# Blocked attention and two MLPs on one core: global queries of 8 heads in 64x32 tiles, local scores in fp32, keys split 96+128, global tokens in the last block

## The chip, the cores and the metric

The kernel runs on one core of a Trainium2 chip. The metric is device time in microseconds (us), the median of three runs: 881.46 us before (879.99 to 882.30). Engines are named as in the profile: PE (TensorE matmul), PEld (its weight loads), DVE (VectorE), ACT (ScalarE), POOL (GpSimd), SP (SyncE, which issues all loads here).

## What is computed

Four batches, eight heads, 512 local and 32 global tokens of head size 64. Global queries look at all 544 keys, local queries at the 32 global keys and at a window of 32 to each side. Two MLPs with a squared ReLU follow, over 2176 tokens (512 to 2048 to 512).

```
s_g = scale * q_g @ concat(k_g, k_l).T;            out_g = softmax(s_g) @ concat(v_g, v_l)
s_ll = where(|i - j| <= 32, scale * q_l @ k_l.T, -1e9);  s_lg = scale * q_l @ k_g.T
out_l = softmax(concat(s_lg, s_ll)) @ concat(v_g, v_l)
x = concat(out_g, out_l) as (B*S, H*D)
x = relu(x @ w_in)**2 @ w_out      # twice, with moe_* and moe2_* weights
```

## The kernel before

Everything is fp32 in and out. An MLP product is done as three fp32r products (`three`, L568: high x high, high x low, low x high), so each operand is split once into a high fp32r part (ACT) and a low rest (DVE). In this text a triple is one call of `three`.

The 2176 tokens stand in five column blocks of 384, 512, 512, 384 and 384. Blocks 1 and 2 form pair A, 3 and 4 pair B; later stages multiply a pair in a Strassen-like scheme (`products`, `tsums`), block 0 plainly (`first`).

**Attention.** `pair(j)` (L309) does two heads for 256 local queries, 32 times. It loads keys, queries and values, splits keys and queries into fp32r parts (`hk`, `lk`, `hq`, `lq`), and computes scores (L338) for two query tiles t and two heads e in 12 matmuls; the heads lie in rows 0-63 and 64-127 and write two PSUM banks, S0 and S1. DVE adds the mask and takes the row extreme (L350), ACT does exp with a row sum (L355), DVE adds 1e-9 and inverts (L360, L361), and a scaling step (`copy("nm")`, L365) normalises. PE transposes the 224 probabilities as 112+112 (L373), ACT brings them from PSUM (`copy("ev")`), PE multiplies by the values (L386) and `split_out` writes `xh` and `xl`.

`glob(n)` (L404) does the global queries of four heads of one batch, eight times: scores with a 128-wide block-diagonal query operand (L426), maximum (L430), exp (L439), normalisation on POOL (L447), transposes (L452, L456), 20 matmuls with values as the stationary operand (L465).

**First wave.** Once all heads of a block's tokens are there, the first four of 16 hidden chunks of MLP 1 run on it: 32 triples for a block, 160 in all. Their weights are made by `weight` (L480) from 8-byte words. This work fills PE between attention steps. Then come 14 stages of two chunks each; only they hold the rest of the time.

**Order.** `Plan.order` (L131) is a list planner: each step has an engine, a cost, a priority and what it reads and writes; the planner simulates the engines and emits a fixed order for each. Engines run their own order and wait on semaphores. `CFG` holds priorities, buffer counts and which engine takes the turn for a copy (`A`, `D`, `P` for ACT, DVE, POOL, in rotation). A load's priority is its user's less `lead`.

Of the kernel before, what the change touches and what calls it, by code (L numbers as in the profile page):

```python
# [17 lines left out]
S = SG + SL  # L18
# [179 lines left out]
def act(n):  # L198
    return 0.055 + 0.835 * n / 1000
# [7 lines left out]
def kernel(ctx: ExitStack, tc: tile.TileContext, kl, ql, vl, gk, gv, win, wout, msk, idn, out):  # L207
# [101 lines left out]
    def pair(j, prio):  # L309
        u, h2 = divmod(j, H // 2)  # L310
        kb, qb, mb, vb = j % NK, j % NQ, j % NM, j % NV
# [3 lines left out]
        def P():  # L315
# [3 lines left out]
        K, Q, M, ML, HQ, LQ = ("rk", kb), ("rq", qb), ("hk", mb), ("lk", mb), ("hq", mb), ("lq", mb)  # L319
# [3 lines left out]
        load(prio - lead + 0.5, vt[vb], vl[j], 229376, A, (("v", vb),))  # L323
        copy("ck", P(), hk[mb], rk[kb], KW, A + (K,), (M,))
        copy("cq", P(), hq[mb], rq[qb], 256, A + (Q,), (HQ,), scalar=-0.125)
        add("DVE", dve(256), P(), lambda: nc.vector.scalar_tensor_tensor(
            out=lq[mb], in0=rq[qb], scalar=-0.125, in1=hq[mb].bitcast(F32),
            op0=ALU.mult, op1=ALU.subtract), A + (Q, HQ), (LQ,), lock=True)
        minus("lo", P(), lk[mb], rk[kb], hk[mb].bitcast(F32), KW, A + (K, M), (ML,))
        sk = [take("S", CFG["S"]) for _ in range(2)]  # L330

        def scores():
            for t in range(2):
                c, w = slice(128 * t, 128 * t + 128), slice(160 * t, 160 * t + WIN)
                for n, (a, b) in enumerate(((hq, hk), (lq, hk), (hq, lk))):
                    for e in range(2):
                        r = slice(64 * e, 64 * e + 64)
                        nc.tensor.matmul(out=bank[sk[e]][:, t * WIN:(t + 1) * WIN], lhsT=a[mb][r, c], rhs=b[mb][r, w],  # L338
                                         start=n == 0, stop=n == 2)

        add("PE", 0.767, P(), scores, A + (M, ML, HQ, LQ), tuple(sk), mode="S")
# [595 lines left out]
```

## Time and profile before

| | before |
|---|---|
| median of three runs | 881.46 us |
| span of the profiled execution | 877.9 us |
| time outside the span (median less span) | 3.6 us |
| PE / DVE / ACT / POOL busy | 867.1 / 695.6 / 539.4 / 47.7 us |
| attention's last matmul ends | 215.4 us |
| first wave ends, the stages go on | about 248.9 us |

The profile gives the profiled execution's span, from its first to its last instruction, and no other time of it. PE's busy time is not a measure of its load, since matmuls overlap and a matmul that waits inside the pipe counts as busy. How much of a stretch a piece of PE work takes is read from the chain of waits, where each piece stands with the time from the end of the piece before it.

### The profile page before, as it was taken

To read this page: it belongs to the slowest core of one execution; us is meant where nothing else is said; L and a number is where in the kernel's file an instruction comes from. 1 tells how busy PE (TensorE), PEld (TensorE's weight loads), DVE (VectorE), ACT (ScalarE), POOL (GpSimd) and SP (SyncE) were. 2 spreads that over 40 slices of the span, in tenths; PEclk is the share of its full clock that TensorE was granted. 3 is DMA by queue.
4 is the path that set the end of the run, shared out by engine and by line. 5 is a ranking of instruction groups with operands and counts; after the bars stand their busy time and mean duration, and the time that the engine had idled before them with its cause. 6 is when DMAs were issued, how large, how long until landed. Compare 5 with 4: busy or idle time off the path is not lost.

```text
span 877.9 us, 14427 instructions
## 1 busy us (share of the span) xinstructions
PE 867.1 (99%) x5294; PEld 769.4 (88%) x5294; DVE 695.6 (79%) x1657; ACT 539.4 (61%) x1219; POOL 47.7 (5%) x94
## 2 busy tenths in 40 slices
PE   8999999999999999999999999999999999999998
PEld 7777787898889989999889889889988989899896
DVE  4899998832999788897968999788787887895654
ACT  5799999964675456355456678745554545644533
POOL 1232222200000000000000000000000000000000
PEclk9999999999999999999999999999999999999999
DMA  9687355400001121120201002211111111210022
GB/s 300 232 292 252 106 153 162 115 12 1 1 25 49 49 67 53 49 69 29 72 25 49 25 25 72 61 60 49 49 49 49 49 49 48 63 58 25 1 100 104
DMA packets 28070, 67.92 MB, mean 77 GB/s; under 512 B 3168, under 2 KB 13024, under 8 KB 28000
## 3 DMA queue, kind: packets, MB, share of 16 engines
q1 hardware_dynamic: 28000, 67.01, 24.0%
q8 instruction: 41, 0.67, 0.3%
q14 instruction: 29, 0.24, 0.1%
HBM read 62.54 MB, written 4.46 MB: 76 GB/s over the span
## 4 chain that ended last, share of the span: by engine, by line
PE 86%; DVE 6%; ACT 4%; DMA 2%; issue 1%; SPq 0%; ACTq 0%; DVEq 0%
PE h L569 8%; PE h L570 7%; PE h L571 7%; PE PT L570 6%; PE PT L571 6%; PE PT L569 6%; PE S L570 5%; PE S L571 5%; PE S L569 5%; PE Y L569 5%; PE Y L570 4%; PE Y L571 4%; PE O L571 3%; PE O L570 3%; PE O L569 3%; PE O L386 3%
## 5 line engine op out<-in xcount | busy, mean ns | idle before, releaser
L238 DVE TENSOR_TENSOR gl<-r,gh 128x384 fp32r<-128x384 f32 (+1 forms) x160 | 96.2, 607 | 61.7 <-ACT r L593 60.3
L589 ACT ACTIVATE r<-r 128x512 f32<-128x512 f32 (+1 forms) x84 | 48.2, 575 | 94.7 <-DVE r L699 94.4
L570 PE MATMUL PT<-gl,whi 128*128 128x384 f32 (+1 forms) x288 | 103.0, 358 | 0.0
L569 PE MATMUL PT<-gh,whi 128*128 128x384 f32 (+1 forms) x288 | 102.9, 357 | 0.0
L571 PE MATMUL PT<-gh,wlo 128*128 128x384 f32 (+1 forms) x288 | 102.9, 357 | 0.0
L524 ACT ACTIVATE whi<-wt 128x512 fp32r<-128x512 f32 x92 | 57.3, 626 | 65.5 <-DVE wt L500 50.4
L590 ACT ACTIVATE gh<-r 128x384 fp32r<-128x384 f32 (+1 forms) x160 | 89.0, 563 | 5.3 <-issue 1.3
L569 PE MATMUL h<-xh,whi 128*128 128x384 f32 (+1 forms) x244 | 88.9, 364 | 0.6 <-DVE xh L226 0.5
L570 PE MATMUL h<-xl,whi 128*128 128x384 f32 (+1 forms) x244 | 86.2, 353 | 0.0
L571 PE MATMUL h<-xh,wlo 128*128 128x384 f32 (+1 forms) x244 | 86.1, 353 | 0.0
L622 DVE TENSOR_TENSOR y<-y,PT 128x384 f32<-128x384 f32 (+1 forms) x130 | 75.6, 601 | 11.3 <-PE PT L571 11.2
L593 ACT ACTIVATE r<-r 128x384 f32<-128x384 f32 (+1 forms) x145 | 82.1, 570 | 3.6
L569 PE MATMUL Y<-gh,whi 128*128 128x384 f32 (+1 forms) x208 | 76.1, 366 | 0.0
L570 PE MATMUL Y<-gl,whi 128*128 128x384 f32 (+1 forms) x208 | 74.7, 359 | 0.3 <-DVE gl L238 0.3
L571 PE MATMUL Y<-gh,wlo 128*128 128x384 f32 (+1 forms) x208 | 74.3, 357 | 0.0
L238 DVE TENSOR_TENSOR wlo<-wt,whi 128x512 fp32r<-128x512 f32 x92 | 62.5, 685 | 6.7 <-ACT whi L524 6.2
L355 ACT ACTIVATE s<-s,mn 128x224 f32<-128x224 f32 x128 | 60.1, 473 | 10.8 <-DVE mn L350 10.5
L571 PE MATMUL S<-xh,wlo 128*128 128x384 f32 (+1 forms) x172 | 62.0, 360 | 0.0
L570 PE MATMUL S<-xl,whi 128*128 128x384 f32 (+1 forms) x172 | 61.9, 360 | 0.0
L569 PE MATMUL S<-xh,whi 128*128 128x384 f32 (+1 forms) x172 | 61.6, 358 | 0.0
L570 PEld LDWEIGHTS PT<-gl,whi 128*128 128x128 f32 x288 | 54.1, 188 | 4.8
L569 PEld LDWEIGHTS PT<-gh,whi 128*128 128x128 f32 x288 | 54.1, 188 | 4.8
(131 smaller groups left out, 2100.1 us busy)
## 6 DMA issues: line engine op xcount, KB each, us to landing
wraw<-win SPq DMA_DIRECT2D x32, 512.0 KB, 3.6
wraw<-wout SPq DMA_DIRECT2D x32, 512.0 KB, 3.5
v<-vl SPq DMA_DIRECT2D x32, 224.0 KB, 3.1
rk<-kl SPq DMA_DIRECT2D x32, 192.0 KB, 2.8
y<-gk SPq DMA_DIRECT2D x8, 672.0 KB, 4.7
y<-gv SPq DMA_DIRECT2D x8, 640.0 KB, 6.3
rq<-ql SPq DMA_DIRECT2D x32, 128.0 KB, 3.0
out<-y SPq DMA_DIRECT2D x12, 192.0 KB, 1.9
```

Of the source, the lines that this page charges most:

```text
L238: add("DVE", dve(n), prio, lambda: nc.vector.tensor_tensor(out=get(out_), in0=get(a), in1=get(b), op=ALU.subtract), reads, writes, lock=True)
L355: add("Activation", 0.48, P(), lambda t=t, sb=sb: nc.scalar.activation(out=st[sb][:, t, :], in_=st[sb][:, t, :], func=AF.Exp, bias=mn[sb][ ...
L386: nc.tensor.matmul(out=bank[ok][64 * e:64 * e + 64, 128 * t:128 * t + 128], lhsT=vt[vb][:, 128 * k + 64 * e:128 * k + 64 * e + 64], rhs=pt ...
L524: nc.scalar.activation(out=whi[slot], in_=tf, func=AF.Copy)
L569: nc.tensor.matmul(out=out_, lhsT=hi, rhs=xhi, start=start, stop=False, skip_group_check=again)
L570: nc.tensor.matmul(out=out_, lhsT=hi, rhs=xlo, start=False, stop=False, skip_group_check=again)
L571: nc.tensor.matmul(out=out_, lhsT=lo, rhs=xhi, start=False, stop=stop, skip_group_check=again)
L589: add("Activation", act(nb), P(), lambda: nc.scalar.activation(out=r, in_=src, func=AF.Relu), (S,), (R,))
L590: add("Activation", act(nb) + 0.04, P(), lambda: nc.scalar.activation(out=a, in_=r, func=AF.Square), (R,), (("gh", f),))
L593: add("Activation", act(nb) + 0.04, P(), lambda: nc.scalar.activation(out=r, in_=r, func=AF.Square), (), (R,))
L622: add("DVE", dve(nb), P(), lambda: nc.vector.tensor_tensor(out=yd, in0=yd, in1=o, op=ALU.add), (yk[d],), (Y,))
```

## The change

Local attention: keys and queries stay fp32. The four splits and their buffers go; two fp32 matmuls (one for each head) replace six fp32r ones for a query tile. The scale -0.125 moves into the DVE step with the mask, whose values become -8e9. One `sm` buffer for both heads replaces three; DVE adds and inverts once for a pair. The scaling step rotates over `DDDADD` in place of `APA`. Probabilities are transposed as 96+128, the smaller part on 96 rows, and leave PSUM in two ACT copies in place of one. `xh` is always made by ACT.

Global attention: `glob` takes all eight heads of a batch, four times. Scores go as eight 64-row, 32-column tiles into both S banks; the value product has probabilities as the stationary operand (32 columns a head, four side by side) and 64 value columns moving; normalisation is done after it, in the ACT copies from PSUM (L480 of the new file), followed by one more transpose. Keys get own tiles `kg`; only the values still borrow `y` tiles. POOL has no work left.

Layout and plan: block 0 becomes the last columns (last unit and all global tokens). Buffers, priorities and the order of blocks within the first wave (`begin`) and within the stages (`order`) change. `fw` 2 means the same four chunks as before. The number of triples is 1224 in both programs.

```diff
@@ -22,59 +22,58 @@
 UNITS = 8
 NI = UNITS * H
 WIN = 224
+NEAR = 96
 KW = 384
 NEG = 1.0e9
 NB = [384, 512, 512, 384, 384]
-OFF = [0, 384, 896, 1408, 1792]
-UNIT0 = [0] + [384 + 256 * u for u in range(UNITS - 1)]
+OFF = [1792, 0, 512, 1024, 1408]
+UNIT0 = [256 * u for u in range(UNITS)]
 GLOB0 = 256
+GLOB_V = (4, 0)
 PAIRS = {"A": (1, 2), "B": (3, 4)}
...
-CFG = {'warm': 23,
+CFG = {'warm': 27,
- 'nm': 'APA',
+ 'nm': 'DDDADD',
- 'glob': [2, 4, 6, 8, 13, 17, 25, 31],
+ 'glob': [5.9, 15.73, 25.15, 42.23],
- 'lmk': -11.49,
+ 'lmk': -15.028,
- 'NM': 2,
- 'NS': 3,
+ 'NM': 1,
+ 'NS': 5,
- 'xh': 'DDADD',
+ 'xh': 'AA',
- 'begin': [1, 0, 3, 4, 2]}
+ 'begin': [1, 2, 4, 3, 0],
+ 'fw': 2}
...
+    sm = tiles(ap_, "sm", NM, [128, 2, 2])
+    kg = tiles(ap_, "kg", 2, [128, 1152 + S])
+    gmx = ap_.tile([128, 2, 2], F32, name="gmx")
+    gsm = ap_.tile([128, 2], F32, name="gsm")
...
-        copy("ck", P(), hk[mb], rk[kb], KW, A + (K,), (M,))
-        copy("cq", P(), hq[mb], rq[qb], 256, A + (Q,), (HQ,), scalar=-0.125)
-        add("DVE", dve(256), P(), lambda: nc.vector.scalar_tensor_tensor(
-            out=lq[mb], in0=rq[qb], scalar=-0.125, in1=hq[mb].bitcast(F32),
-            op0=ALU.mult, op1=ALU.subtract), A + (Q, HQ), (LQ,), lock=True)
-        minus("lo", P(), lk[mb], rk[kb], hk[mb].bitcast(F32), KW, A + (K, M), (ML,))
+        load(prio - lead + 0.5, vt[vb], vl[j], 262144, A, (("v", vb),))
         sk = [take("S", CFG["S"]) for _ in range(2)]
 
         def scores():
             for t in range(2):
                 c, w = slice(128 * t, 128 * t + 128), slice(160 * t, 160 * t + WIN)
...
+                for e in range(2):
+                    r = slice(64 * e, 64 * e + 64)
+                    nc.tensor.matmul(out=bank[sk[e]][:, t * WIN:(t + 1) * WIN], lhsT=rq[qb][r, c], rhs=rk[kb][r, w],
+                                     start=True, stop=True)
+
+        add("PE", 0.77, P(), scores, A + (K, Q), tuple(sk), mode="S")
...
                     out=st[sb][:, t, :], in0=bank[s][:, t * WIN:(t + 1) * WIN], in1=masks[:, mi, :],
-                    op0=ALU.add, op1=ALU.min, scale=1.0, scalar=3.0e38, accum_out=mn[sb][:, t:t + 1]),
+                    op0=ALU.add, op1=ALU.min, scale=-0.125, scalar=3.0e38, accum_out=mn[sb][:, t:t + 1]),
...
-                    accum_out=sm[sb][:, t:t + 1]), A + (("mn", sb, t),), (("s", sb, t), ("sm", sb, t)))
-
...
+        def tiny():
+            nc.vector.tensor_scalar_add(out=sm[mb], in0=sm[mb], scalar1=1e-9)
+            nc.vector.reciprocal(out=sm[mb], in_=sm[mb])
+
+        add("DVE", 0.3, P(), tiny, A, tuple(("sm", mb, e, t) for e in range(2) for t in range(2)), lock=True)
+        for e in range(2):
+            i = 2 * j + e
+            sb = i % NS
             for t in range(2):
-                copy("nm", P(), st[sb][:, t, :], st[sb][:, t, :], WIN, A + (("sm", sb, t),), (("s", sb, t),),
-                     scalar=sm[sb][:, t:t + 1])
+                copy("nm", P(), st[sb][:, t, :], st[sb][:, t, :], WIN, A + (("sm", mb, e, t),), (("s", sb, t),),
+                     scalar=sm[mb][:, e, t:t + 1])
             tk = take("PT", CFG["PT"])
 
             def trans(sb=sb, tk=tk):
                 for t in range(2):
...
+                    nc.tensor.transpose(bank[tk][:, 256 * t:256 * t + 128], st[sb][:, t, NEAR:WIN], ident)
+                    nc.tensor.transpose(bank[tk][0:NEAR, 256 * t + 128:256 * t + 128 + NEAR],
+                                        st[sb][0:NEAR, t, 0:NEAR], ident[0:NEAR, 0:NEAR])
+
+            add("PE", 0.384, P(), trans, A + (("s", sb, 0), ("s", sb, 1), "ident"), (tk,), mode="T")
             pb = i % NPT
-            copy("ev", P(), pt[pb][0:112, :], bank[tk][0:112, :], 512, A + (tk,), (("pt", pb),), psum=True)
+            two = bank[tk].rearrange("p (t c) -> p t c", t=2)
+            copy("ev", P(), pt[pb][:, :, 0:128], two[:, :, 0:128], 256, A + (tk,), (("pt", pb),), psum=True)
+            copy("ev", P(), pt[pb][0:NEAR, :, 128:128 + NEAR], two[0:NEAR, :, 128:128 + NEAR], 2 * NEAR, A + (tk,), (("pt", pb),), psum=True)
             pbs.append(pb)
 
         def pv():
             for t in range(2):
-                for c in range(2):
+                for n, c in ((128, 1), (NEAR, 0)):
                     k = 2 * t + c
                     for e in range(2):
...
+                        nc.tensor.matmul(out=bank[ok][64 * e:64 * e + 64, 128 * t:128 * t + n],
+                                         lhsT=vt[vb][0:n, 128 * k + 64 * e:128 * k + 64 * e + 64],
+                                         rhs=pt[pbs[e]][0:n, t, 128 - 128 * c:128 - 128 * c + n], start=c == 1, stop=c == 0,
+                                         skip_group_check=True)
+
+        add("PE", 0.817, P(), pv, A + (("pt", pbs[0]), ("pt", pbs[1]), ("v", vb)), (ok,), mode="V")
...
-    def glob(n, prio):
...
+    def glob(bb, prio):
         A = ("arena",)
...
+        K, V = kg, [yflat[b] for b in GLOB_V]
+        GK, GP, GV = [("gk", 0), ("gk", 1)], [("gp", 0), ("gp", 1)], [("gv", 0), ("gv", 1)]
+        p = [k[:, 1152:1152 + S] for k in K]
+        rem, og = K[0][0:32, 512:768], K[1][:, 512:640]
+        ok = CFG["O"][cnt["g"] % len(CFG["O"])]
...
+        for g in range(2):
+            load(prio - 3 + 0.05 * g, K[g][:, 0:1152], gk[2 * bb + g], 589824, A, (GK[g], GP[g]))
+        for g in range(2):
+            load(prio - 2.9 + 0.05 * g, V[g][:, 0:1280], gv[2 * bb + g], 655360, A, (GV[g],))
         for e in range(2):
...
+            sk = [take("S", CFG["S"]) for _ in range(2)]
 
             def scores(sk=sk, e=e):
...
+                for g in range(2):
+                    for j in range(2):
+                        c = 32 * (2 * g + j)
+                        for r in range(2):
+                            rows = slice(64 * r, 64 * r + 64)
+                            nc.tensor.matmul(out=bank[sk[r]][c:c + 32, 0:272], lhsT=K[g][rows, 1088 + 32 * j:1120 + 32 * j],
+                                             rhs=K[g][rows, S * j + 272 * e:S * j + 272 * e + 272], start=True, stop=True)
+
+            add("PE", 0.47, P(), scores, A + tuple(GK), tuple(sk), mode="X")
+            for r in range(2):
+                add("DVE", 0.37, P(), lambda s=sk[r], e=e, r=r: nc.vector.tensor_tensor_reduce(
+                    out=p[r][:, 272 * e:272 * e + 272], in0=bank[s][:, 0:272], in1=zeros, op0=ALU.add, op1=ALU.max,
+                    scale=1.0, scalar=-3.0e38, accum_out=gmx[:, r, e:e + 1]), A + (sk[r], "masks"), (GP[r], "gmx"))
...
+        for r in range(2):
+            add("Activation", 0.75, P(), lambda r=r: nc.scalar.activation(
+                out=p[r], in_=p[r], func=AF.Exp, bias=gmx[:, r, 0:1], scale=0.125, accum_out=gsm[:, r:r + 1]),
+                A + ("gmx",), (GP[r], ("gsm", r)))
...
+        for r in range(2):
+            tk = take("PT", CFG["PT"])
+
+            def trans(r=r, tk=tk):
+                for c in range(4):
+                    nc.tensor.transpose(bank[tk][:, 128 * c:128 * c + 128], p[r][:, 128 * c:128 * c + 128], ident)
+
+            add("PE", 0.436, P(), trans, A + (GP[r], "ident"), (tk,), mode="T")
+            copy("ev", P(), K[r][:, 0:512], bank[tk], 512, A + (tk,), (GK[r],), psum=True)
+        tk = take("PT", CFG["PT"])
+
+        def trans_rem(tk=tk):
+            for r in range(2):
+                nc.tensor.transpose(bank[tk][0:32, 128 * r:128 * r + 128], p[r][:, 512:544], ident)
+
+        add("PE", 0.218, P(), trans_rem, A + (GP[0], GP[1], "ident"), (tk,), mode="T")
+        copy("ev", P(), rem, bank[tk][0:32, 0:256], 256, A + (tk,), (GK[0],), psum=True)
 
         def pv():
...
+            for c0, c1 in ((0, 4), (4, 5)):
+                for r in range(2):
+                    for c in range(c0, c1):
+                        for t in range(4):
+                            g, j = divmod(t, 2)
+                            lhs = K[r][:, 128 * c + 32 * t:128 * c + 32 * t + 32] if c < 4 else rem[:, 128 * r + 32 * t:128 * r + 32 * t + 32]
+                            v = V[g][0:128 if c < 4 else 32, 256 * c + 64 * (2 * j + r):256 * c + 64 * (2 * j + r) + 64]
+                            nc.tensor.matmul(out=bank[ok][32 * t:32 * t + 32, 64 * r:64 * r + 64], lhsT=lhs, rhs=v,
+                                             start=c == 0 and r == 0, stop=c == 4, skip_group_check=True)
+
+        add("PE", 1.2, P(), pv, A + tuple(GK) + tuple(GV), (ok,), mode="W")
+        for r in range(2):
+            add("Activation", act(64) + 0.1, P(), lambda r=r: nc.scalar.activation(
+                out=og[:, 64 * r:64 * r + 64], in_=bank[ok][:, 64 * r:64 * r + 64], func=AF.Copy, scale=gsm[:, r:r + 1]),
+                A + (ok, ("gsm", r)), (GK[1],))
+        add("PE", 0.109, P(), lambda: nc.tensor.transpose(bank[ok][:, 128:256], og, ident), A + (GK[1], "ident"), (ok,), mode="T")
         c0 = GLOB0 + 32 * bb
...
+        split_out(0, range(KD), xh[0][:, :, c0:c0 + 32], xl[0][:, :, c0:c0 + 32],
+                  ok, bank[ok][:, 128:256].rearrange("p (a q) -> p a q", a=KD), 128, P)
...
-                first = {1: (("gk", 0), ("gp", 0)), 2: (("gk", 1), ("gp", 1)), 3: (("gv", 0),), 4: (("gv", 1),)}.get(b, ())
+                first = (("gv", GLOB_V.index(b)),) if b in GLOB_V else ()
...
+    FW = CFG["fw"]
+    W = weights(range(2 * FW), CFG["w0"], CFG["w1"], False)
     for j in range(NI // 2):
...
-        for n in range(4):
+        for n in range(2 * FW):
             first(P, W, b, n, n, i == 4)
-        second(P, b, range(4), W["out"], i == 4, i != 4, (0, True, False))
+        second(P, b, range(2 * FW), W["out"], i == 4, i != 4, (0, True, False))
...
-    msk = np.stack([np.where(glob | (near & ok), 0.0, NEG) for ok in (pos >= 0, pos > -99, pos < 128)], axis=1)
+    msk = np.stack([np.where(glob | (near & ok), 0.0, -8 * NEG) for ok in (pos >= 0, pos > -99, pos < 128)], axis=1)
```

How the change moves PE's instructions, local attention first. Before, the first pair's scores, transposes and value product (S, PT and O are PSUM banks):

```order
L338 MATMUL S_150<-hk_119,hq_123 128x224
L338 MATMUL S_151<-hk_119,hq_123 128x224
L338 MATMUL S_150<-hk_119,lq_125 128x224
L338 MATMUL S_151<-hk_119,lq_125 128x224
L338 MATMUL S_150<-lk_121,hq_123 128x224
L338 MATMUL S_151<-lk_121,hq_123 128x224
...
L373 MATMUL PT_152<-ident,s_127 112x128 x4
...
L386 MATMUL O_154<-pt_130,v_133 64x128
L386 MATMUL O_154<-pt_131,v_133 64x128
```

The same pair in the changed kernel:

```order
L327 MATMUL S_149<-rk_115,rq_118 128x224
L327 MATMUL S_150<-rk_115,rq_118 128x224
...
L363 MATMUL PT_151<-ident,s_123 128x128
L364 MATMUL PT_151<-ident,s_123 96x96
...
L379 MATMUL O_153<-pt_128,v_131 64x128
L379 MATMUL O_153<-pt_129,v_131 64x128
L379 MATMUL O_153<-pt_128,v_131 64x96
L379 MATMUL O_153<-pt_129,v_131 64x96
```

Three matmuls for a head and query tile became one that reads the loaded tiles, and half of the transposes and value products became 96 wide.

PE, one global step of four heads before:

```order
L426 MATMUL S_150<-y_76 128x272 x2
L452 MATMUL PT_152<-ident,y_75 128x128 x4
L456 MATMUL PT_153<-ident,y_75 32x128
L426 MATMUL S_151<-y_76 128x272 x2
L373 MATMUL PT_152<-ident,s_128 112x128 x4
L465 MATMUL O_154<-y_75,y_77 64x32 x20
```

A global step of eight heads in the changed kernel (rows of local attention between them left out):

```order
L425 MATMUL S_149<-kg_139 32x272
L425 MATMUL S_150<-kg_139 32x272
...
L425 MATMUL S_149<-kg_140 32x272
L425 MATMUL S_150<-kg_140 32x272
...
L454 MATMUL PT_151<-ident,kg_139 128x128 x4
L454 MATMUL PT_152<-ident,kg_140 128x128 x4
...
L462 MATMUL PT_151<-ident,kg_139 32x128
L462 MATMUL PT_151<-ident,kg_140 32x128
...
L475 MATMUL O_153<-y_78,kg_139 32x64 x2
L475 MATMUL O_153<-y_74,kg_139 32x64 x2
...
L483 MATMUL O_153<-ident,kg_140 128x128
```

Scores come in groups of eight that fill both S banks, twice a step; 40 value matmuls follow one another on bank O.

SP, the first loads of the program before:

```order
L306 DMA rk_114<-kl 128x384
L306 DMA rq_116<-ql 128x256
L306 DMA v_133<-vl 112x512
L306 DMA rk_115<-kl 128x384
L306 DMA rq_117<-ql 128x256
L306 DMA v_134<-vl 112x512
L306 DMA masks<-msk 128x672
L306 DMA rq_118<-ql 128x256
```

And now:

```order
L302 DMA rk_115<-kl 128x384
L302 DMA rq_118<-ql 128x256
L302 DMA masks<-msk 128x672
L302 DMA v_131<-vl 128x512
L302 DMA rk_116<-kl 128x384
L302 DMA rq_119<-ql 128x256
L302 DMA v_132<-vl 128x512
```

The masks moved from the seventh to the third load. The identity went from the twelfth to the thirteenth.

## Rows read from the trace of the kernel before

**Rows 1.** Busy time by stretch: from:to length, PE, PEld, DVE, ACT, POOL, clock, DMA
```profile
0.00:12.50 12.50, 10.55 (x71) 9.79 (x72) 4.94 (x20) 3.76 (x11) 2.68 (x10) 1.00 0.84 243
12.50:75.00 62.50, 58.81 (x656) 45.35 (x656) 54.92 (x237) 53.65 (x162) 17.42 (x31) 0.97 0.80 276
75.00:215.40 140.40, 139.93 (x1226) 116.46 (x1226) 100.24 (x416) 119.97 (x353) 27.55 (x54) 1.00 0.36 109
215.40:248.90 33.50, 32.93 (x160) 28.82 (x161) 30.04 (x53) 21.95 (x42) 0.00 (x0) 1.00 0.00 1
248.90:874.00 625.10, 624.70 (x3184) 568.93 (x3182) 504.82 (x934) 340.05 (x654) 0.00 (x0) 1.00 0.16 51
```

**Rows 2.** The chain of waits, 3 to 50 us: start, us, what
```profile
3.53 5.92 DMA masks<-msk
9.59 0.39 DVE s L350
...
49.06 0.99 ACT s L355 x5
```

**Rows 3.** The chain of waits, 100 to 115 us
```profile
100.01 0.86 PE S L338 x12
100.87 0.43 PE h L569
101.30 0.23 PE h L570
...
101.77 0.44 PE PT L373 x4
...
102.91 0.92 PE S L426 x4
103.83 1.02 PE O L386 x16
104.85 1.11 PE S L426 x4
...
107.78 0.58 PE PT L373 x4
...
113.06 1.64 PE O L465 x40
```

**Rows 4.** Timeline of PE, two query tiles' scores; starts that follow closely are merged
```profile
99.94 0.37 PE L338 MATMUL S<-hk,hq 64*128 64x224 f32 x2
100.15 0.28 PE L338 MATMUL S<-hk,lq 64*128 64x224 f32 x2
100.27 0.27 PE L338 MATMUL S<-lk,hq 64*128 64x224 f32 x2
```

**Rows 5.** Timeline of PE, the global value product, cut at 60.50 us
```profile
60.19 0.54 PE L465 MATMUL O<-y,y 128*64 128x32 f32 x11
```

**Rows 6.** ACT up to 215.4 us by line: busy, mean ns, idle before
```profile
L223 ACT ACTIVATE s<-s,sm 128x224 f32<-128x224 f32 x85 | 38.5, 474 | 4.2 <-DVE sm L361 3.7
L223 ACT ACTIVATE pt<-PT 112x512 f32<-112x512 f32 x64 | 36.3, 586 | 3.4 <-PE PT L373 3.0
L223 ACT ACTIVATE hk<-rk 128x384 fp32r<-128x384 f32 x18 | 9.2, 513 | 0.0
```

**Rows 7.** DVE up to 215.4 us by line
```profile
L238 DVE TENSOR_TENSOR lk<-rk,hk 128x384 fp32r<-128x384 f32 x32 | 18.0, 563 | 2.7 <-POOL hk L231 2.7
L326 DVE SCALAR_TENSOR_TENSOR lq<-rq,hq 128x256 fp32r<-128x256 f32 x32 | 13.6, 425 | 0.4 <-POOL hq L231 0.4
L226 DVE CAST xh<-O 128x256 fp32r<-128x256 f32 (+2 forms) x34 | 11.9, 354 | 12.6 <-PE O L386 11.4 <-PE O L465 0.9
L361 DVE RECIPROCAL sm<-sm 128x2 f32<-128x2 f32 x64 | 10.6, 166 | 2.2
```

**Rows 8.** The chain of waits, the last 14 us
```profile
865.89 0.50 PE Y L570
...
874.18 0.69 DVE y L622
```

More of the change, by code (lines that the diff above doesn't have):

```diff
@@ L334, in scores @@
                 c, w = slice(128 * t, 128 * t + 128), slice(160 * t, 160 * t + WIN)
[L335 to L341, printed above, removed]
+                for e in range(2):
[3 more added lines that the diff above has]
+        add("PE", 0.77, P(), scores, A + (K, Q), tuple(sk), mode="S")
         pbs = []
         ok = CFG["O"][j % len(CFG["O"])]
+        mb = j % NM
         for e in range(2):
-            i = 2 * j + e
-            sb, s = i % NS, sk[e]
+            sb, s = (2 * j + e) % NS, sk[e]
             for t in range(2):
@@ L424, in scores @@
             def scores(sk=sk, e=e):
-                for pr in range(2):
-                    nc.tensor.matmul(out=bank[sk][:, 0:272], lhsT=k[:, 1088 + 128 * pr:1216 + 128 * pr],
-                                     rhs=k[:, S * pr + 272 * e:S * pr + 272 * e + 272], start=pr == 0, stop=pr == 1)
-            add("PE", 0.917, P(), scores, A + (GK,), (sk,), mode="T")
-            add("DVE", 0.37, P(), lambda sk=sk, e=e: nc.vector.tensor_tensor_reduce(
-                out=p[:, 272 * e:272 * e + 272], in0=bank[sk][:, 0:272], in1=zeros, op0=ALU.add, op1=ALU.max,
-                scale=1.0, scalar=-3.0e38, accum_out=gmx[:, e:e + 1]), A + (sk, "masks"), (GP, "gmx"))
+                for g in range(2):
[5 more added lines that the diff above has]
+                                             rhs=K[g][rows, S * j + 272 * e:S * j + 272 * e + 272], start=True, stop=True)
@@ L444, in tsum @@
             nc.vector.reciprocal(out=gsm, in_=gsm)
-        add("DVE", 0.3, P(), tsum, A, ("gsm",), lock=True)
-        add("Pool", 0.72, P(), lambda: nc.gpsimd.tensor_scalar(
-            out=p, in0=p, scalar1=gsm, scalar2=0.0, op0=ALU.mult, op1=ALU.add), A + ("gsm",), (GP,))
-        def trans():
-            for c in range(4):
-                nc.tensor.transpose(bank[t1][:, 128 * c:128 * c + 128], p[:, 128 * c:128 * c + 128], ident)
-        add("PE", 0.436, P(), trans, A + (GP, "ident"), (t1,), mode="T")
@@ L455, in glob @@
-        copy("ev", P(), kt[:, 0:512], bank[t1], 512, A + (t1,), (GK,), psum=True)
-        add("PE", 0.06, P(), lambda: nc.tensor.transpose(bank[t2][0:32, 0:128], p[:, 512:544], ident),
-            A + (GP, "ident"), (t2,), mode="T")
-        copy("ev", P(), kt[0:32, 512:640], bank[t2][0:32, 0:128], 128, A + (t2,), (GK,), psum=True)
-        def pv():
-            for j0 in (0, 2):
-                for c in range(5):
-                    kc = 128 if c < 4 else 32
-                    for j in (j0, j0 + 1):
-                        nc.tensor.matmul(
-                            out=bank[ok][64 * (j % 2):64 * (j % 2) + 64, 32 * (j // 2):32 * (j // 2) + 32],
-                            lhsT=v[0:kc, 256 * c + 64 * j:256 * c + 64 * j + 64],
-                            rhs=kt[0:kc, 128 * c + 32 * j:128 * c + 32 * j + 32], start=c == 0, stop=c == 4)
@@ L470, in glob @@
-        add("PE", 1.546, P(), pv, A + (GK, GV), (ok,), mode="W")
+        add("DVE", 0.3, P(), tsum, A, (("gsm", 0), ("gsm", 1)), lock=True)
+        for r in range(2):
[5 more added lines that the diff above has]
+            copy("ev", P(), K[r][:, 0:512], bank[tk], 512, A + (tk,), (GK[r],), psum=True)
@@ L806 @@
         for p in range(STAGES):
-            if layer == 0 and p < 2:
+            if layer == 0 and p < FW:
                 continue
@@ L911, in _order @@
 def _order():
[L912 to L917 removed]
+    local = [S * (u // 2) + SG + 256 * (u % 2) + np.arange(256) for u in range(UNITS)]
+    return np.concatenate(local + [S * b + np.arange(SG) for b in range(B)])
 def kernel(q_l, k_l, v_l, q_g, k_g, v_g, moe_w_in, moe_w_out, moe2_w_in, moe2_w_out):
```

120 lines of the change are left out of this document (38 added, 82 removed).

## The prediction

> **What bounds the kernel now.** First the busy time by stretch. From 248.9 us to 874.0 us PE is busy 624.70 of 625.10 us [rows 1]: the stages have no idle PE time to win or hide anything in, and their 1224 triples less the first wave's 160 are in both programs. What the change can move lies before 248.9 us. There PE, ACT and DVE are all near full: ACT 53.65 and DVE 54.92 of 62.5 us between 12.5 and 75 us, ACT 119.97 of 140.4 us up to the end of attention, PE 139.93 [rows 1]. So I read the chain of waits next. At first it runs through the masks' load and ACT [rows 2]; by 100 us it is PE work from piece to piece [rows 3]: a shorter PE piece brings all behind it forward, as long as ACT and DVE keep up. After attention only 50 first-wave triples are left (the 160 matmuls of 215.4 to 248.9 us, three each).
>
> **PE, term by term.** Prices are chain pieces [rows 3]; the sum is made against this execution's span, 877.9 us, to which 3.6 us outside it are added at the end, so that it stands at the median of 881.46 us.
>
> *Local transposes.* Four take 0.44 us (0.58 behind a change of tile shape, whose 0.14 stays). Two of the four become 96 columns in place of 128: 0.44 x (128+96)/256 = 0.385. 64 groups x 0.055 = -3.5 us; no less than 0 and no more than that, since nothing is added.
>
> *Local values.* 16 records in 1.02 us, of which I take 0.15 as the change of tile shape, like the 0.14 above, and 0.87 as columns. Half of them lose a quarter: 0.87/8 = 0.11, or 0.13 if the whole 1.02 shrinks. 32 x 0.12 = -3.8 us.
>
> *Local scores.* 12 fp32r matmuls take 0.86 us. The trace has no fp32 matmul in row halves. Its nearest is the global scores': four records (an fp32 matmul leaves two) of 272 columns in 0.92 us, 0.23 each, so 0.19 for 224 columns. Eight records become four rounds if the two heads' halves run side by side, as they do in fp32r: two starts stand in one row, and rows follow at 0.11 to 0.12 us, not twice that [rows 4]. 4 x 0.19 = 0.76, plus 0.2 on entering the shape (the first row lasts 0.21 where others last 0.12): 0.96. 32 x 0.10 = +3.2 us. Bounds: without the entry 0.76, -3.2 us; halves one after the other 8 x 0.19 + 0.2 = 1.72, +27.5 us. I take +3.2, the reading by the rows on both sides (fp32 values in two column halves also overlap: 16 records of 128 columns would take 1.7 us alone, by 0.23 for 272, and take 1.02).
>
> *Global scores.* Sixteen groups of four, 0.92 or 1.11 us, mean 1.02: 16.2 us. Now eight groups of 16 records in eight tiles. If all tiles run side by side, a tile's two records are 0.46; with 0.1 for issuing 16 and 0.2 entry 0.76, x8 = 6.1: -10.1 us. If only two ever overlap, as the rows show at most, 16 x 0.23/2 + 0.2 = 2.0, x8 = 16.3: 0. I take -10.1, as every tile that is there overlaps in [rows 4, 5], and keep 0 as the end. The new shape also makes what follows wait: the piece after scores takes 0.43 in place of 0.23 [rows 3], 0.2 x 8 = +1.6, against four shape changes fewer at the value product, -0.8.
>
> *Global values.* Eight times 1.64 us: 13.1. Here 11 starts stand within 0.31 us, 28 ns each, two tiles of 64 columns at once [rows 5]: a round of two takes 0.056. The new step has 80 records of 64 moving columns in 20 rounds of four. By columns a round is 64 x 0.23/272 = 0.054, so it can be no faster than the old round; 20 x 0.056 + 0.35 for entry and the change to 32 rows = 1.5, x4 = 6.0: -7.1 us. At 28 ns a record 2.24 + 0.35 = 2.6, -2.7 us; at the whole step's pace (1.64/40 = 41 ns) 3.5, +0.9 us. I take -7.1.
>
> The Trainium skill ("TensorE: Matmul & The Clock Gate", "Wait — 56ns, not 53.3ns?") says that start to start never drops below about 25 ns however small the matmul is. The 28 ns above agree with such a floor, though they can as well be one round of 56 ns. By that rule the value step is 80 x 0.025 + 0.35 = 2.35, 3.4 us more in all (an estimate); it is a rival below. The same page ("The mechanism") says weight loads overlap running matmuls only in another row group; the four column tiles share theirs. Rows speak against it: the local values, two column tiles in one row group, leave no room for serial weight loads in 1.02 us. I give that no chance.
>
> *Rest.* Four last transposes, about 0.6 us with their shape change: +0.6.
>
> Sum: -3.5 - 3.8 + 3.2 - 10.1 + 1.6 - 0.8 - 7.1 + 0.6 = -19.9 us.
>
> **Start.** DVE's first score step waits for the masks: issued at 3.53 us, landed 5.92 us later, DVE starts at 9.59 [rows 2]. Now two loads in place of six precede them (0.33 of 1.11 MB; 0.78 MB less at the 243 MB/ms of the first stretch [rows 1] is 3.2 us). The scores no longer wait for splits. But the first transposes need the identity, now one load later. I take -2 us of the possible 0 to -3.2.
>
> **ACT and DVE, the cover.** ACT, busy 177.4 us to the end of attention: the scaling step falls from 85 to 21 copies, -30; key copies -9 [rows 6]; 64 extra evictions, each pair of copies some 0.05 dearer than one, +3; 30 `xh` copies at the 0.354 that DVE takes for them, +11 [rows 7]; with 62 rather than 110 triples done by then (PE's order puts the other 98 behind attention) some -8. That leaves about 145 us. DVE, 160 us: -18 -13.6 -11.9 for splits and `xh`, -11 for half of the two small steps, +27 for 107 scalings at 0.25 (halfway between a 0.17 small step and 0.354): about 133 us [rows 7]. 98 triples behind attention take 13 x 0.69 + 85 x 0.52 = 53 us (0.23 a matmul at 512 columns [rows 3], 0.17 at 384 by columns; 13 and 85 are counted in PE's order). If the first wave is to end at 248.9 - 21.9 = 227 us, attention ends at 174 and from 10 us on ACT needs 145 of 164 us, 88%; it has 85% now over the whole stretch [rows 1]. That is tight.
>
> The change also adds a wait: with one `sm` buffer, the next pair's exp may write a sum only after the last pair's scaling has read it. Behind a waiting exp stand ACT's evictions, for which PE's value products wait. The ring: four exps 1.9 us, two small DVE steps 0.34, a scaling 0.25, hand-overs about 0.3: 2.8 us a pair, against some 5 us that a pair now takes (174/32). It fits unless DVE puts a weight step between. For tightness and ring I add +2 us, between -6 (the waits of 12.5 to 75 us shrink with DVE's load) and +16 (half a us a pair).
>
> **Where nothing is lost or won.** The stages' orders change, but each stage keeps its triples; tail: the last wait for `gl` makes a matmul 0.50 in place of 0.23, and DVE's last add is 0.69 [rows 8]; the program now ends on a 384 block with the same chain. 0, within -1 and +3 (an order that makes PE wait at the border of the layers).
>
> Total -19.9 - 2 + 2 = -19.9; 877.9 - 19.9 + 3.6 = **861.6 us**.
>
> **Rivals.**
> 1. *Waits go too:* early ACT and DVE stalls shrink, since splits leave DVE and four global steps no longer crowd the first pairs. Speaks for it: the chain lies on ACT and DVE before 75 us. Against: PE has less to fill with there. -6 in place of +2: 853 us, or less.
> 2. *Issue floor* of the value step: 3.4 us more, 865.0 us.
> 3. *Tiles overlap only in twos:* global scores +10.1, values up to +8: 870 to 880 us.
> 4. *ACT and the sm ring set attention's pace:* +16 in place of +2: 875.6 us. PE's shorter pieces turn into idle time before each exp-fed transpose. For it: ACT is within 12% of full. Against: ring 2.8 of 5 us.
> 5. *Slower: fp32 row halves don't overlap.* Local scores 1.72 in place of 0.96, 32 x 0.76 = +24.3, global scores (two row halves of four columns) +3.7: 889.6 us. It decides once more than 20/28 of the overlap is missing. Against: fp32r halves and fp32 column halves both overlap [rows 3, 4].
>
> **Chances.** Forecast (857 to 864.9) 0.42, rival 1 0.17, rival 2 0.12, rival 3 0.11, rival 4 0.12, rival 5 0.06. A change under 0.3% (2.6 us) can't be told from none. Faster: the forecast, rivals 1 and 2, 0.09 of rival 3 and 0.06 of rival 4, together 0.86. Within 0.3%: 0.02 of rival 3, 0.04 of rival 4 and 0.01 of rival 5, where half of the overlap is there, 0.07. Slower: 0.02 of rival 4 and 0.05 of rival 5, 0.07. Range 849 to 874: it leaves out the far part of rival 1 below and, above, rival 5 and the ends of 3 and 4.
>
> **What would show it.** Local scores at 0.9 to 1.0 us in the chain (1.7 would be rival 5). Global scores at about 0.8 and value steps at 1.5 (2.4 the floor; 2 and 2.6 to 3.5 rival 3). DVE's first score step near 6.5 us. Attention's last matmul near 174 us, the first wave's end near 227, and 625 us of stages behind it. Long waits of ACT's exp for the scaling step, with PE idle at transposes, would be rival 4. The forecast is wrong if the stages take more than 628 us, or if PE's terms come true and attention still ends after 185 us.

## The result and the profile after

The changed kernel takes 854.57 us (854.22 to 856.56, four runs), the kernel before 880.73 us on the same chip: ratio 0.9713, 95% interval 0.9692 to 0.9733. The profiled span falls from 877.9 to 852.7 us, by 25.2 where the forecast had 19.9. The time lies inside the range of 849 to 874, 7.0 us below the forecast of 861.6 and below the forecast's own stretch of 857 to 864.9; rival 1, at 853, stands nearer.

Busy time of the new kernel by stretch, columns as in [rows 1]. The cuts are the same events: attention's last matmul now ends at 168.6 us (215.4 before).

```profile
0.00:12.50 12.50, 11.46 (x81) 10.18 (x82) 4.34 (x25) 6.63 (x22) 0.20 (x4) 1.00 0.78 249
12.50:75.00 62.50, 58.28 (x720) 41.67 (x721) 54.31 (x235) 57.27 (x199) 0.00 (x0) 1.00 0.77 273
75.00:168.60 93.60, 93.08 (x960) 72.30 (x958) 77.43 (x324) 88.19 (x308) 0.00 (x0) 1.00 0.52 168
168.60:224.50 55.90, 55.73 (x300) 52.81 (x301) 28.45 (x51) 30.87 (x62) 0.00 (x0) 1.00 0.03 10
224.50:848.70 624.20, 623.54 (x3187) 569.92 (x3185) 503.59 (x926) 337.82 (x649) 0.00 (x0) 1.00 0.14 50
```

Against [rows 1]: the stages' stretch is as long as it was (624.20 and 625.10 us, PE busy all but 0.7 and 0.4 us of it). The gain is made ahead of it. PE's clock, 0.97 on the mean in 12.5 to 75 us before, is 1.00. ACT is busy 88.19 of 93.60 us from 75 us to attention's end, 94%, where it was 85% (119.97 of 140.40). But that 85% is a mean over a longer stretch. In the same 75 to 168.6 us the kernel before shows

```profile
75.00:168.60 93.60, 93.15 (x892) 74.71 (x893) 84.25 (x350) 91.32 (x274) 24.47 (x47) 1.00 0.51 156
```

so ACT was at 98% there, and its slack came after 168.6 us. In this stretch ACT and DVE are less full now than they were (88.19 for 91.32 and 77.43 for 84.25 us); only between 12.5 and 75 us is ACT fuller (57.27 for 53.65).

A cut by events can mislead here, since the new order leaves 300 matmuls of MLP work between attention's end and 224.5 us, where there were 160. So I compare at equal work: when have the matmuls of the triples done 208,896 columns, the content of the first wave? At 246.97 us before, at 222.57 us after, 24.4 us earlier. At 700,000 columns it is 23.9, at the last matmul 25.5 us (874.1 and 848.6 us).

The chain of waits of the new kernel (start, us, what), at its start, at 40 to 55 us, one load further on, and at its end:

```profile
4.77 0.96 PE S L327 x8
...
11.24 10.18 DMA wraw<-win
...
32.40 8.88 DMA v<-vl
...
41.33 0.99 PE O L379 x16
42.32 0.62 PE S L425 x16
42.94 0.26 PE PT L363
43.20 0.09 PE PT L364
43.28 0.11 PE PT L363
...
43.90 0.92 PE O L379 x16
...
48.18 0.59 PE PT L454 x4
48.77 0.96 PE S L327 x8
49.73 0.43 PE h L581
50.15 0.23 PE h L582
...
53.02 1.39 PE O L475 x80
...
85.21 7.62 DMA v<-vl
...
844.35 0.45 PE Y L582
...
847.10 2.13 DVE y L634 x4
```

Each new piece can be laid beside its old one in [rows 3]. Local scores 0.96 (0.86), local values 0.92 (1.02), a full and a 96-column transpose 0.11 + 0.09 (two of four in 0.44), global scores 0.62 for eight heads, the global value step 1.39 for eight heads (1.64 for four). What the change of tile shape makes late is there too: the first h matmul behind scores takes 0.43, the next 0.23. Until 41 us the chain also runs through two loads; from there to 168.6 us it is PE's work but for one more value load at 85.21 us.

One line's instructions, count, shortest/median/longest ns and first to last start (us): the score steps of DVE in the first 16 us, then one global value step and one global score step:

```profile
L339 DVE CUSTOM_DVE_ANT_0 s<-S,masks x12: 383/387/392, 5.8 to 14.3; 128x224 f32<-128x224 f32 x12
...
L475 PE MATMUL O<-y,kg x80: 214/219/243, 52.9 to 54.2; 128*32 128x64 f32 x64, 32*32 32x64 f32 x16
...
L425 PE MATMUL S<-kg x16: 389/401/413, 42.2 to 42.5; 64*32 64x272 f32 x16
```

DVE's first score step starts at 5.8 us; it was 9.59 behind the masks [rows 2]. The sixteen records of a global score step start within 0.3 us, though each lasts 0.40: eight start about 7 ns apart, and 0.2 us later the other eight (the middle values of all steps). The eight tiles do run side by side.

ACT and DVE up to 168.6 us by line (count, busy us and mean ns of one, idle before and its releasers):

```profile
L222 ACT ACTIVATE pt<-PT 128x256 f32<-128x256 f32 x64 | 22.3, 374 | 0.7 <-PE PT L364 0.5
L222 ACT ACTIVATE pt<-PT 96x192 f32<-96x192 f32 x64 | 18.2, 320 | 0.0
L222 ACT ACTIVATE s<-s,sm 128x224 f32<-128x224 f32 x21 | 10.1, 481 | 3.0 <-DVE sm L350 2.9
...
L227 DVE TENSOR_SCALAR s<-s,sm 128x224 f32<-128x224 f32 x107 | 29.2, 332 | 0.4
```

Two of ACT's waits from 5 to 170 us (us in total, times, longest):

```profile
ACT s L344 <- DVE mn L339: 5.0, 3, 4.3
...
ACT s L344 <- DVE s L227: 2.2, 5, 0.8
```

The scaling on DVE is 0.332 us, not the 0.25 taken (107 of them: 8.8 us more on DVE), and two evictions together cost 0.694 in place of 0.586 [rows 6], 0.11 dearer where 0.05 was taken. The exp's wait for the scaling step, the mark of rival 4, is 2.2 us in all.

### The profile page after: what moved, and what is told of

Read it like the earlier page. It is cut to its first block, busy times and chain, and to the rows that moved or that the text cites. A ratio compares the mean times of both kernels' runs of the same rounds, so it can differ in the third digit from the quotient of the medians.

```text
span 852.7 us, 14049 instructions
## 1 busy us (share of the span) xinstructions
PE 842.1 (99%) x5242; PEld 746.9 (88%) x5242; DVE 668.6 (78%) x1558; ACT 520.8 (61%) x1238; POOL 0.2 (0%) x4
## 4 chain that ended last, share of the span: by engine, by line
PE 91%; DMA 3%; DVE 3%; ACT 2%; issue 1%; SPq 0%; ACTq 0%
PE h L581 8%; PE h L583 7%; PE h L582 7%; PE PT L583 6%; PE PT L582 6%; PE PT L581 6%; PE S L581 5%; PE S L583 5%; PE S L582 5%; PE Y L581 5%; PE Y L582 5%; PE Y L583 5%; PE O L583 3%; PE O L582 3%; PE O L581 3%; PE O L379 3%
## 5 line engine op out<-in xcount | busy, mean ns | idle before, releaser
L602 ACT ACTIVATE gh<-r 128x384 fp32r<-128x384 f32 (+1 forms) x146 | 81.6, 562 | 8.6 <-PE O L583 5.0
L581 PE MATMUL h<-xh,whi 128*128 128x384 f32 (+1 forms) x216 | 79.6, 368 | 0.0
L583 PE MATMUL h<-xh,wlo 128*128 128x384 f32 (+1 forms) x216 | 77.9, 361 | 0.0
L582 PE MATMUL h<-xl,whi 128*128 128x384 f32 (+1 forms) x216 | 77.6, 359 | 0.0
L601 ACT ACTIVATE r<-r 128x512 f32<-128x512 f32 (+1 forms) x70 | 40.2, 574 | 53.8 <-DVE r L711 53.7
L583 PE MATMUL S<-xh,wlo 128*128 128x384 f32 (+1 forms) x200 | 70.1, 350 | 0.0
L581 PE MATMUL S<-xh,whi 128*128 128x384 f32 (+1 forms) x200 | 70.0, 350 | 0.0
L582 PE MATMUL S<-xl,whi 128*128 128x384 f32 (+1 forms) x200 | 69.9, 350 | 0.0
L583 PEld LDWEIGHTS PT<-gh,wlo 128*128 128x128 f32 x288 | 54.1, 188 | 4.5
```

Of the source, the lines that this page charges most:

```text
L581: nc.tensor.matmul(out=out_, lhsT=hi, rhs=xhi, start=start, stop=False, skip_group_check=again)
L582: nc.tensor.matmul(out=out_, lhsT=hi, rhs=xlo, start=False, stop=False, skip_group_check=again)
L583: nc.tensor.matmul(out=out_, lhsT=lo, rhs=xhi, start=False, stop=stop, skip_group_check=again)
L601: add("Activation", act(nb), P(), lambda: nc.scalar.activation(out=r, in_=src, func=AF.Relu), (S,), (R,))
L602: add("Activation", act(nb) + 0.04, P(), lambda: nc.scalar.activation(out=a, in_=r, func=AF.Square), (R,), (("gh", f),))
```

## The experiments

The theory: the time up to the first wave's end is PE's own work, so shorter pieces pass through. The rivals: ACT and DVE, or the `sm` ring, set the pace; or it isn't the pieces but the plan that was renewed with them. Ratios are against the kernel before on the same chip, with 95% intervals; after itself stands at 0.9713, span 852.7 us.

### Which engine sets the pace: work added, order unchanged

Every local score matmul issued twice (the second writes the same values again; the planner's cost is left as it was, so all else keeps its place):

```diff
                     nc.tensor.matmul(out=bank[sk[e]][:, t * WIN:(t + 1) * WIN], lhsT=rq[qb][r, c], rhs=rk[kb][r, w],
                                      start=True, stop=True)
+                for e in range(2):
+                    r = slice(64 * e, 64 * e + 64)
+                    nc.tensor.matmul(out=bank[sk[e]][:, t * WIN:(t + 1) * WIN], lhsT=rq[qb][r, c], rhs=rk[kb][r, w],
+                                     start=True, stop=True)
```

> The changed kernel with every local score matmul issued twice into the same place; the order of all steps is unchanged, ACT and DVE do the same work. The second set is 4 rounds of 0.19 us a pair, 32 x 0.76 = 24.3 us of PE work and of nothing else. Theory (up to the end of the first wave the time is PE's own work, so a piece removed from PE comes off the total): 22 to 25 us slower than the changed kernel, 877 to 880 us. Rival (ACT and DVE set the pace of attention, and PE's pieces lie beside them): the added PE work falls into PE's idle time, at most 10 us slower, under 865 us.

875.96 us, ratio 0.9967 (0.9952 to 0.9982), span 874.2. The chain of waits of this kernel shows what was added to a pair:

```profile
102.70 0.58 PE S L327 x4
103.28 0.38 PE S L331 x4
103.66 0.38 PE S L327 x4
104.03 0.38 PE S L331 x4
```

That is 1.72 us in place of 0.96; 32 x 0.76 = 24.3 us. Of it 21.5 us, 88%, appear in the span, 20.8 of them by the first wave's end: just under the theory's 22 to 25 us and far above the rival's 10. (It is also just what rival 5 would have cost, had the halves not overlapped.)

One more ACT copy, then instead one more DVE addition, for each head of a pair (behind the second exp and the second mask step; they read only the masks and nothing reads them):

```diff
+                    if t == 1:
+                        nc.scalar.activation(out=junk[:, 0:WIN], in_=masks[:, 1, :], func=AF.Copy)
```

> The changed kernel with 64 more ACT copies of 128x224 (one behind the second exp of each head, from the masks into a tile that nobody reads), 0.37 us each: 23.7 us of ACT work during attention and nothing for PE. Theory (PE's own work is the limit): 0 to 6 us slower, 854 to 861 us, since attention may end later as long as first-wave triples fill PE. Rival (ACT sets attention's pace): 16 to 24 us slower, 871 to 879 us.

> The changed kernel with 64 more DVE additions of 128x320 elements (one behind the second masking step of each head, from the masks into a tile that nobody reads), 0.35 to 0.42 us each: 22 to 27 us of DVE work during attention and nothing for PE. Theory (PE's own work is the limit): 0 to 6 us slower, 854 to 861 us. Rival (DVE's relief from the splits is what made the change faster): 12 to 24 us slower, 867 to 879 us.

ACT: 64 copies of 0.383 us, 24.5 us, gave 862.71 us (0.982, 0.9804 to 0.9837), span +8.7. DVE: 64 additions of 0.486 us, 31.1 us, gave 866.41 us (0.9861, 0.9842 to 0.988), span +11.8. Neither figure is what a side had expected: 36% and 38% pass through. Busy time with more ACT work, 75 to 168.6 us:

```profile
75.00:168.60 93.60, 92.06 (x923) 69.67 (x922) 76.78 (x327) 90.89 (x333) 0.00 (x0) 1.00 0.54 171
```

And with more DVE work, from 12.5 us:

```profile
12.50:75.00 62.50, 56.62 (x670) 39.69 (x667) 57.59 (x236) 52.71 (x186) 0.00 (x0) 0.95 0.74 260
75.00:168.60 93.60, 90.62 (x916) 67.70 (x916) 88.91 (x358) 81.86 (x289) 0.00 (x0) 1.00 0.54 171
```

ACT is at 97% and DVE at 95% after 75 us, and PE has begun to lose (92.06 and 90.62 of 93.60, 93.08 without); DVE's work also brought a clock of 0.95 ahead of it. PE's records come in the same order in all three runs. So in after's order work added to PE passes through by 88%, work added to ACT or DVE by a little over a third: PE is the limit, and the other two stand right behind it. Rival 4 named ACT rightly as near its limit, but not the price.

### Buffers

A third buffer for local values (`NV` 3), since the chain waits 8.88 us for `v` at 32.4 us; then the same with the planner's loads taken as slower (290e3 bytes a us in place of 360e3); then a second `sm` buffer (`NM` 2), which takes the ring of rival 4 away.

```diff
- 'NV': 2,
+ 'NV': 3,
...
- 'NM': 1,
+ 'NM': 2,
```

> The changed kernel with three value buffers in place of two; the planner orders anew. In the changed kernel's chain a value load issued at 32.4 us lands 8.9 us later, behind global loads, and PE's wasted time is largest before 50 us (12 us between 12.5 and 50). If such late loads make a good part of it: 2 to 5 us faster, 850 to 853 us. If ACT and DVE make it: within 1 us of 854.6.

> The changed kernel with three value buffers and a planner that counts loads at 290 in place of 360 bytes per ns (the trace moves 249 to 273 GB/s in the first 75 us). The program differs in order alone. If the planner's too fast loads cause the waits before 50 us: 2 to 6 us faster than the changed kernel, 849 to 853 us. If not, within 2 us of 854.6, or slower where tuned priorities no longer fit.

> After with two sm buffers in place of one. If the ring of the one buffer sets attention's pace (rival 4): 846 to 851 us, attention's last matmul 4 to 8 us earlier. If it doesn't: within 853 to 862 us, as the order is planned anew and other small changes of the plan cost up to 5 us.

859.62 us (0.9787, 0.9771 to 0.9802), 860.01 us (0.9782, 0.9762 to 0.9803) and 862.44 us (0.9813, 0.9798 to 0.9827): all slower than after, by 4.8 to 8.8 us of span. Each setting also made the planner write a new order: 1483, 1620 and 1454 of PE's 5242 matmuls now stand where after has another one. With the third value buffer PE is busy 56.76 us of 12.5 to 75 us (58.28 without). I lay the loss to the new orders, since more room should cost nothing by itself; no run shows that apart. So what late value loads or the ring cost can't be told from these runs. In after's trace ACT's waits for the scaling step are the 2.2 us above.

### Parts of the change in the old plan

The fp32 local scores alone, put into the kernel before:

```diff
-        copy("ck", P(), hk[mb], rk[kb], KW, A + (K,), (M,))
...
-                for n, (a, b) in enumerate(((hq, hk), (lq, hk), (hq, lk))):
-                    for e in range(2):
...
+                for e in range(2):
+                    nc.tensor.matmul(out=bank[sk[e]][:, t * WIN:(t + 1) * WIN], lhsT=rq[qb][r, c], rhs=rk[kb][r, w],
+                                     start=True, stop=True)
```

> The kernel before with one part of the change: local scores as two fp32 matmuls for a query tile, the four splits gone, all else as before (scaling on ACT and POOL, two global steps a batch, 112+112 keys). PE gains 0.10 us a pair (0.96 in place of 0.86), DVE loses some 32 us of splits and ACT some 9. Theory (PE's own work is the limit): the relief of DVE and ACT is worth little; -4 to +4 us against the kernel before, 877 to 885 us. Rival (relief of ACT and DVE made the change faster): 10 to 20 us faster, 861 to 871 us.

890.58 us, ratio 1.0138 (1.0109 to 1.0167): slower, which neither side had. The step costs PE 32 x 0.10 = 3.2 us, the span grows 8.7. Attention ends 30 us earlier (185.3 us), and the triples come later: 60,000 columns are done at 176.5 us in place of 158.1, 208,896 with 4.2 us and 300,000 with 8.2 us delay. So the planner, free of the splits, put attention ahead of the work that filled PE before; that this order starves PE is what the delay suggests, and no run takes it apart.

The new global step alone in the kernel before, at 4, 8, 17 and 31, and then, from there, at after's positions:

```diff
- 'glob': [2, 4, 6, 8, 13, 17, 25, 31],
+ 'glob': [4, 8, 17, 31],
...
-    def glob(n, prio):
+    def glob(bb, prio):
```
```diff
- 'glob': [4, 8, 17, 31],
+ 'glob': [5.9, 15.73, 25.15, 42.23],
```

> The kernel before with the other large part alone: a global step takes the eight heads of a batch in 64x32 tiles, four times, at the second of each pair of old places. Read from the changed kernel's trace, PE's global work falls from 37.9 to 19.9 us and DVE and ACT lose about 5 and 0. Theory (PE's own work is the limit): 14 to 19 us faster than before, 862 to 867 us. Rival (the gain came from the splits and from where the steps run): less than 6 us faster, 875 us or more.

> Before with the new global step, now at after's positions 5.9, 15.73, 25.15 and 42.23 in place of 4, 8, 17 and 31. If crowding of the global steps into the first pairs made that version lose 24 us: 865 to 890 us, with most of the idle PE time of 12.5 to 75 us gone. If the splits and the scaling on POOL and the old buffers do it wherever the steps stand: 895 to 910 us.

904.78 us (1.0294, 1.0272 to 1.0315) and 894.85 us (1.0183, 1.0145 to 1.0221). A step whose pieces save PE some 17 us made the kernel 24.7 us of span longer. It isn't quite after's step: here it borrows `y` tiles for its keys too, so that one step takes the tiles between which two old steps alternated, while after has own `kg` tiles. What that costs wasn't tested. Busy time by stretch with the steps at 4, 8, 17 and 31:

```profile
12.50:50.00 37.50, 31.03 (x341) 20.62 (x341) 30.71 (x119) 27.67 (x83) 6.43 (x11) 0.77 0.74 252
50.00:75.00 25.00, 18.08 (x252) 12.67 (x251) 19.01 (x76) 18.62 (x58) 5.05 (x10) 0.86 0.64 203
```

PE's longest sums of waits in this kernel (us in total, times, longest):

```profile
PE PT L373 <- ACT s L223: 7.4, 13, 1.7
PE PT L373 <- POOL s L231: 6.3, 6, 4.4
PE O L386 <- ACT pt L223: 3.1, 4, 1.4
```

PE is idle 13.4 of these 62.5 us, 10.6 of them behind these three, the scaling of probabilities on ACT and POOL and an eviction, and its granted clock is 0.77 and 0.86: half speed (1.2 GHz) for 17.1 us from 33.1 us and 6.8 us from 67.2 us. The kernel before has 3.4 us of half clock there, after has none. So a gap is paid as idle time, and part of the work behind it at half speed. After's positions bring back 10 of the 25 us, by the medians, and land between the two expectations; PE is still idle 11.3 us of 12.5 to 75 us, so most of the idle time there has another cause than the positions.

### Code and plan crossed

After's code with before's first-wave numbers; after's code with before's global positions alone; before's code with after's numbers (its eight global steps in twos at after's positions, and after's order of blocks). Buffer counts, the turns of the engines and the stages' order stay with the code, and the first keeps after's order of blocks (`begin`), so its plan isn't wholly before's. The diff is that of the first:

```diff
- 'glob': [5.9, 15.73, 25.15, 42.23],
- 'w0': 26.27364175797601,
...
- 'moe': [65.961, 79.468, 82.888, -1123.016, 96.609],
+ 'glob': [4, 8, 17, 31],
+ 'w0': 19597.98,
...
+ 'moe': [1102.105, 55.352, -324.586, -428.236, -5.672],
```

> After's code with before's first-wave numbers (global steps at 4, 8, 17 and 31, and before's moe, step, w0, w1, lid, lmk and lead). If the gain is in the shorter PE pieces alone and the plan hardly matters: 853 to 859 us. If the plan has to feed PE, as the two single code parts in the old plan suggest (890.6 and 904.8 us): 862 to 890 us, with PE idle before 100 us and the same loss at the first wave's end.

> After with the global steps alone put back to 4, 8, 17 and 31. If their place makes most of the 31 us by which the old numbers are slower (two of the four fall into the first eight steps): 868 to 886 us. If the MLP's and the loads' priorities make it: 854 to 864 us.

> Before's code with after's first-wave numbers: global steps in twos at 5.9, 15.73, 25.15 and 42.23, and after's moe, step, w0, w1, lid, lmk, lead and order of blocks. If the new numbers are simply the better plan for any code: 860 to 876 us. If each set of numbers fits only its own code: 880 to 905 us, with PE idle before 100 us.

| code | first-wave numbers | us | ratio (95%) | 208,896 columns at |
|---|---|---|---|---|
| before | before's | 880.73 | 1 | 246.97 us |
| before | after's | 903.39 | 1.0284 (1.0253 to 1.0316) | 264.9 us |
| after | before's | 885.84 | 1.0073 (1.0054 to 1.0091) | 253.8 us |
| after | before's positions only | 868.05 | 0.9862 (0.9847 to 0.9878) | 235.4 us |
| after | after's | 854.57 | 0.9713 (0.9692 to 0.9733) | 222.57 us |

After's code with before's numbers is slower than before, with every short piece in its chain (0.96, 0.62, 1.39). Its busy time by stretch:

```profile
12.50:50.00 37.50, 30.35 (x346) 18.80 (x348) 26.33 (x109) 25.35 (x88) 0.00 (x0) 0.91 0.70 251
50.00:75.00 25.00, 22.96 (x275) 16.70 (x263) 18.78 (x81) 21.38 (x73) 0.00 (x0) 0.93 0.64 217
75.00:100.00 25.00, 21.57 (x253) 16.28 (x251) 20.18 (x91) 23.17 (x81) 0.00 (x0) 1.00 0.73 243
```

From 12.5 to 100 us PE is busy 74.88 of 87.5 us, ACT 69.90 and DVE 65.29: none is full over the whole, and PE's clock is down to 0.91 and 0.93. Behind attention, which ends at 194.2 us, PE is idle for 7.9 us more (7.2 between 12.5 and 50 us), mostly waiting for ACT's evictions of MLP results (busy time, then the wait):

```profile
200.00:250.00 50.00, 42.07 (x198) 35.74 (x198) 26.47 (x45) 23.67 (x47) 0.00 (x0) 0.97 0.10 32
...
PE Y L581 <- ACT y L222: 7.4, 6, 2.9
```

The positions alone make 13.2 of the 33.3 us of span by which it is slower than after. The new numbers aren't a better plan for any code either: before's code loses 2.8% with them. They fit the code that they were made for.

## Why the prediction was right

What the pieces show up to 208,896 columns. "Own" is the undisturbed step in the chain times the number of steps (0.86 us x 32 to 0.96 us x 32 for the local scores); "with waits" counts each matmul's time from the end of the one before it to its own:

| term | forecast | own | with waits |
|---|---|---|---|
| local transposes | -3.5 | 27.9 to 25.2, -2.7 | -4.2 |
| local values | -3.8 | 32.6 to 29.4, -3.2 | -4.2 |
| local scores | +3.2 | 27.5 to 30.7, +3.2 | +3.3 |
| global scores | -10.1 | 14.7 to 5.0, -9.7 | -12.3 |
| global values | -7.1 | 13.1 to 5.5, -7.6 | -7.6 |
| global transposes | +0.6 | 4.4 to 4.8, +0.4 | +1.8 |
| first-wave triples | 0 | 0 | -1.5 |

*PE's terms* came out: -19.6 us of own work against -20.7 forecast. The two choices that carried the sum held. Row halves overlap in fp32 (rival 5 falls: eight records in 0.96 us), and all eight or four tiles that are there run side by side (rival 3 falls: 0.62 and 1.39 us, not 2.0 and 2.6). That each of these microseconds comes off the total, as the argument has it, is what the doubled scores bear out, at 88%.

*The step that was mis-sized* is the cover: what ACT, DVE and the shape changes take from PE. Shape changes, waits and start were forecast as +1.6 - 0.8 + 2 - 2 = +0.8. All time up to 208,896 columns that isn't own work went from 32.3 to 27.5 us, -4.8. The start came out: 10.8 to 8.8 us in the first 12.5 us, -2.0, with DVE's first score step 3.8 us and PE's first transpose 1.9 us earlier. The rest, forecast as +2.8, is about -2.8: between 12.5 and 50 us it rose from 7.7 to 10.6, and after that it fell from 13.8 to 8.0. If the shape changes cost their +0.8, that leaves -3.6 for tightness, where I allowed +2 and rival 1 had -6. So more than half of rival 1 happened, though not where it looked first: the waits before 50 us grew. Which part of the change took the later ones away no run shows.

The term of 3.6 us outside the span was 1.9, so that of the 7.0 us between forecast and time 5.3 lie in the span and 1.7 here. ACT's load was put at 145 us to attention's end and is 152 (6.63 + 57.27 + 88.19), DVE's at 133 and is 136; attention still ended at 168.6, not 174. The engines were fuller than I took them to be, and it did no harm in this order. The copies that I added show that there was little left: of 24.5 us more on ACT and 31.1 us more on DVE a little over a third passes through.

*Issue floor* (rival 2): 80 records of the value step in 1.39 us are 17.4 ns each. By the rule of the Trainium skill ("TensorE: Matmul & The Clock Gate", "Wait — 56ns, not 53.3ns?"), about 25 ns from start to start, it would have been 2.0 us without the entry; the trace disagrees, and the measurement decides. The trace of before could have settled it: the old step's starts stand about 7 and 51 ns apart in turn, so the 28 ns were a mean of rounds and no floor.

*Stages:* "0, within -1 and +3" was -1.1 at the last matmul; the tail gave 0.3 back, with four last DVE adds in the chain where there was one [rows 8].

*What the prediction had not seen* is how much its argument leaned on the order. It treated PE's shorter pieces as time won as long as the cover holds. The doubled scores show that this is so within after's order; the crossed runs show that the same pieces in another order win nothing. I read the new order's quality from no row; that it fed PE as well as the old one was luck for the forecast. Why one order feeds PE and another starves it was seen only as waits, not taken apart: which of the other numbers (`moe`, `w0`, `w1`, loads) makes the remaining 20 us stays open.

## What to carry to other kernels

A shorter piece on the bounding engine is worth its length only in an order that still feeds the engine: double one piece without touching the order and see how much passes through. Where a planner writes the order, one part of a change tried alone tests the planner as much as the part; cross code and plan numbers to tell them apart. Small fp32 products can be packed by tiles: price them by the rounds of all tiles, plus 0.15 to 0.2 us for each change of shape, as here.

## What the runs showed of the hardware

- Eight 64x32 fp32 tiles overlap in full: 16 records of 272 columns in 0.62 us, entry included; a lone record took 0.23 us [rows 3].
- Four tiles of 128x32 started 80 records at 17.4 ns each, though each record lasts 0.22 us.
- Half clock came after PE had gaps in early attention: 3.4 us in all in the kernel before, 24 us up to 75 us in the version with the new global step alone, where PE was busy 31.03 of 37.5 us.
- DVE's scaling of 128x224 by a column took 332 ns; on ACT a plain copy of that size took 383 ns and the scaling 481 ns.
